# Polysketch attention and a gated feed-forward layer on one core: w_out of the first two blocks narrowed separately, later range limits taken one slot later, and the first keys' features made pair by pair

## The chip, the cores and the metric

The kernel runs on one core of a Trainium2 chip. The metric is the device time of one execution in microseconds (us). A core has five engines that run side by side, each through its own list of instructions in order: PE (TensorE, matrix products into PSUM; its weight loads are a row of their own in the profile, PEld), DVE (VectorE), ACT (ScalarE), POOL (GpSimd) and SP, which issues DMAs here. Engines wait for one another on semaphores.

## The reference

For each of 4 batches and 4 heads there are 1088 tokens with queries, keys and values of 32 numbers. With two small matrices S1 and S2 (8 x 32), features are made: phi(x) holds the 64 products of (S1 x) and (S2 x). Then

```
kv  = sum over tokens of phi(k) v          z = sum over tokens of phi(k)
x   = (phi(q) kv) / (phi(q) z + 1e-6)      heads side by side: 4352 tokens x 128
out = (sigmoid(x w_gate) * (x w_val)) w_out     128 -> 1536 -> 128
```

S1, S2 and the three feed-forward weights arrive as 64-bit floats, q, k and v as 32-bit ones.

## The kernel before

**Attention**, batch by batch. Keys and queries are turned by DVE (turn_k, turn_q). kps makes the sketches of the keys with eight matmuls of 64 x 32 weights: four groups of tokens, and two pairs of heads (pi) in each. Both pairs go into one PSUM tile of two banks (`t[:, pi]`), and DVE turns each pair back into KAB. outer multiplies KAB into the key features KP; for batch 0 gram gets the sum z early, from the products of KAB with itself. kv0 (batch 0) or kv sums kv, and dn makes denominators and numerators; DVE divides and writes xT, the input of the feed-forward layer. A batch's queries come in two parts; the second part's features (batch 0) travel through DRAM (q01, qcomp and spread) and are multiplied by qmult, L630.

**Feed-forward**, over 9 chunks of tokens (512 each, the last 256), and in each over 12 blocks of 128 hidden units. w1 (L351) is a wave: gate and value of one block, 4 passes of 512 columns on PE (L363), then the sigmoid on ACT (L371). glu multiplies the two on DVE (L384), one slot later. w2 (L320, tile moeout) adds the block's share of the output, another slot later. slot (L398) writes this order: the pending glu, the due w2, the next w1. Work of later batches is put into slots of earlier chunks. All orders on PE, DVE, ACT and POOL are the order of the program text.

**Narrowing.** The 64-bit weights are loaded as pairs of words and brought to 32-bit floats on the chip, in the first chunk while the waves run. A block j takes w_gate, w_val and w_out together (384 columns). narrow (L83) is a generator with four steps:

- step 0: POOL limits the high word (L97, tile cap); ACT converts the low word (L101, tile tail)
- step 1: DVE shifts and joins bits of the high word (L105, L109, tile head)
- step 2: ACT squares the limited value (L117, tile square); POOL adds tail to head (L118)
- step 3: DVE writes the weight, with values below a bound set to zero (L127, tile w_sb)

The square goes to a PSUM bank if one is named (`bank`), else it is written over cap in SBUF. Blocks 10 and 11 have no bank. In this text "part" numbers are those of narrow_01 (L187), which narrows blocks 0 and 1: part 0 is gate and value of block 0, part 1 those of block 1, and part 2 is w_out of both blocks at once (256 columns). Parts 0 and 1 and the first steps of part 2 and block 2 stand around the division of the first tokens (head1, L871). The rest is issued by w1 (L372 to L379): in the slot of wave j0 of chunk 0, step 3 of block j0 + 1, steps 1 and 2 of block j0 + 2, and step 0 of block j0 + 4. head1 issues step 0 of blocks 2 and 3.

PSUM tiles are taken by tag: "acc0" and "acc1" (one bank each; output sums, squares and small results), "two" (two banks) and "wave" (two tiles of two banks).

Of the kernel before, what the change touches and what calls it, by code (L numbers as in the profile page):

```python
# [8 lines left out]
F32 = mybir.dt.float32  # L9
# [7 lines left out]
P = 128  # L17
# [3 lines left out]
def kernel(  # L21
# [12 lines left out]
    nc = tc.nc  # L34
# [11 lines left out]
    NJK = 9  # L46
    KBASE = [0, 9, 17, 25]
    assert T == 34
    TCH = 512
# [12 lines left out]
    pso = ctx.enter_context(tc.tile_pool(name="pso", bufs=1, space=bass.MemoryType.PSUM))  # L62
# [112 lines left out]
    def narrow_w(j, step):  # L175
        if not 0 <= j < NJ:
            return
        n, jj = divmod(j, 2)
        if wide:
            if step == 0:  # L180
                narrowing[j] = narrow(
                    w_sb[:, :, j, :], w_in[n][:, :, jj], nc.gpsimd, "acc1" if j < NJ - 2 else None
                )
            next(narrowing[j])


    def narrow_01(part, step):  # L187
        if wide:
            if step == 0:
                i = (slice(0, 2), part) if part < 2 else (2, slice(0, 2))  # L190
                narrowing["01", part] = narrow(
                    w_sb[:, i[0], i[1]],
                    w_in[0][:, i[0], i[1]],
                    nc.gpsimd,
                    "acc0" if part else "acc1",
                )
            next(narrowing["01", part])

# [81 lines left out]
    for c in range(2):  # L280
        rows = slice(64 * c, 64 * c + 64)
        nc.vector.tensor_reduce(
            out=m_col[rows, c],
            in_=ident[rows].rearrange("p (k j) -> p j k", j=R),
# [3 lines left out]
    for t, x in (  # L288
# [5 lines left out]
        out=e_sum,  # L294
        in_=bass.AP(
            tensor=e_row.tensor,
            offset=e_row.offset,
            ap=[list(e_row.ap[0]), [0, 2], [1, R], [0, R]],
        ),
# [4 lines left out]
    for n in range(2):  # L304
        t = const.tile([P, H, 32], F32, tag=f"zb{n}", name=f"zb{n}")
# [45 lines left out]
    def w1():  # L351

        ci = moe["ci"]
        t0, tw = tok_chk[ci]
        jn = TCH // tw
        j0 = moe["w"] * jn
        wv = psm.tile([P, 2, TCH], F32, tag="wave", name="wave")

        tp = tw // 2 if ci == 0 and j0 == 0 else tw
        for o in range(0, tw, tp):  # L360
            for which in range(2):
                for jj in range(jn):
                    nc.tensor.matmul(  # L363
                        out=wv[:, which, jj * tw + o : jj * tw + o + tp],
                        lhsT=w_sb[:, which, j0 + jj, :],
                        rhs=xT[:, t0 + o : t0 + o + tp],
                        start=True,
                        stop=True,
                    )
        sg = sbG.tile([P, TCH], F32, tag="sg", name="sg", bufs=3)  # L370
        nc.scalar.activation(out=sg, in_=wv[:, 0], func=ACTF.Sigmoid)  # L371
        if ci == 0:  # L372
            if j0 == 1:
                narrow_01(2, 3)
            if 0 < j0 < NJ - 2:
                narrow_w(j0 + 1, 3)
            narrow_w(j0 + 2, 1)
            narrow_w(j0 + 2, 2)
            narrow_w(j0 + 4, 0)  # L379


        def glu():
            g = sbG.tile([P, TCH], F32, tag="g", name="g")
            nc.vector.tensor_tensor(out=g, in0=wv[:, 1], in1=sg, op=MUL)  # L384
            moe["todo"].append((ci, j0, jn, g.rearrange("p (j t) -> p j t", j=jn)))

        moe["gate"] = glu
        moe["w"] += 1
        if j0 + jn == NJ:
            moe["ci"] += 1  # L390
            moe["w"] = 0
# [29 lines left out]
    kT_of, qT_of = {}, {}  # L421
# [22 lines left out]
    KP, QP, BQ, ND, KAB, ASB, KVZ, KVD, Z4, ZS = ({} for _ in range(10))  # L444

    def kps(b):
        t = ps2.tile([P, 2, 512], F32, tag="two", name="kps")
        for g in range(4):
            for pi in range(2):
                rows = slice(64 * pi, 64 * pi + 64)  # L450
                nc.tensor.matmul(  # L451
                    out=t[32 * g : 32 * g + 32, pi, : NJK * 32],
                    lhsT=sk[rows, :],
                    rhs=kT_of[b][rows, KBASE[g] : KBASE[g] + NJK],
                    start=True,
                    stop=True,
                )

        KAB[b] = sbA.tile([P, 2, NJK, 32], F32, tag="kab", name="kab")
        for pi in range(2):  # L460
            nc.vector.transpose(
                out=KAB[b][:, pi].rearrange("p j c -> p (j c)"), in_=t[:, pi, : NJK * 32]
            )
        KP[b] = sbA.tile([P, 2, NJK, 2, F], F32, tag="kp", name="kp")

    def gram():
        t = pso.tile([P, TCH], F32, tag="acc1", name="gram")
        for pi in range(2):  # L470
            for j in range(NJK):
                g = 32 * (j % 4)
                x = KAB[0][: 64 if j == 0 else P, pi, j]
                nc.tensor.matmul(  # L474
                    out=t[g : g + 32, 32 * pi : 32 * pi + 32],
                    lhsT=x,
                    rhs=x,
                    start=(j < 4),
                    stop=(j >= NJK - 4),
                    skip_group_check=True,  # L480
                )
        gs = const.tile([P, 2, 2, 2, R], F32, tag="gs")
        nc.scalar.copy(out=gs.rearrange("p a m x r -> p (a m x r)"), in_=t[:, :64])
        gh = const.tile([P, 2, 2, R], F32, tag="gh")
        nc.gpsimd.tensor_tensor(
            out=gh,
            in0=gs[:, :, :, 1],
            in1=bass.AP(
                tensor=e_m.tensor,
                offset=e_m.offset,  # L490
                ap=[list(e_m.ap[0]), [0, 2], [1, 2], [0, R]],
            ),
            op=MUL,
        )

        def spread_z():
            nc.tensor.matmul(
                out=t[:, 64 : 64 + H * R],
                lhsT=e_sum.rearrange("p c i j -> p (c i j)"),
                rhs=gh.rearrange("p a m r -> p (a m r)"),  # L500
                start=True,
                stop=True,
            )

        def mask_z():
            zm = const.tile([P, H, 2, R], F32, tag="zm")
            z0 = t[:, 64 : 64 + H * R]
            nc.vector.tensor_tensor(
                out=zm,
                in0=bass.AP(  # L510
                    tensor=z0.tensor, offset=z0.offset, ap=[list(z0.ap[0]), [R, H], [0, 2], [1, R]]
                ),
                in1=bass.AP(
                    tensor=m_col.tensor,
                    offset=m_col.offset,
                    ap=[list(m_col.ap[0]), [0, H], [R, 2], [1, R]],
                ),
                op=MUL,
            )
            nc.vector.tensor_reduce(  # L520
                out=zb[0][:, :, :2], in_=zm, axis=mybir.AxisListType.X, op=ALU.add
            )

        return spread_z, mask_z
# [268 lines left out]
    else:  # L793
        nc.vector.tensor_copy(
            out=s4[:, 1:],
            in_=bass.AP(
                tensor=s4.tensor, offset=s4.offset, ap=[list(s4.ap[0]), [0, 3], [1, D]]
            ),
# [5 lines left out]
        out=st_[:, : 2 * R],  # L804
        lhsT=s4.rearrange("p g d -> p (g d)"),
        rhs=ident[: 2 * R, : 2 * R],
        is_transpose=True,
        start=True,
        stop=True,
# [3 lines left out]
    sk = const.tile([P, 2, 2, R], F32, tag="sk")  # L813
    nc.vector.tensor_tensor(
        out=sk,
# [11 lines left out]
    sk = sk.rearrange("p m n r -> p (m n r)")  # L827
    sab = []
    for n, inner in enumerate(([[1, R], [0, R]], [[0, R], [1, R]])):
        t = const.tile([P, R, R], F32, tag=f"s{n}", name=f"s{n}")  # L830
        s0 = st_[:, n]
        nc.scalar.copy(
            out=t, in_=bass.AP(tensor=s0.tensor, offset=s0.offset, ap=[list(s0.ap[0])] + inner)
        )
        sab.append(t.rearrange("p i j -> p (i j)"))
    sa, sb = sab
    turn_q(0, 0)
    kps(0)
    ab((0, 0, 0))
    ab((0, 1, 0))  # L840
    spread_z, mask_z = gram()
    mult00 = ab(None, (0, 0, 0))
    mult10 = ab(None, (0, 1, 0), (psm, "wave"))
    for part in range(2):
        narrow_01(part, 0)
# [25 lines left out]
    def head1():  # L871
        narrow_01(1, 1)
        narrow_01(0, 3)
        narrow_01(1, 2)
        narrow_01(2, 0)
        narrow_w(2, 0)
        narrow_w(3, 0)

    divide((0, 4), (4, 8), between=head1)
    narrow_01(1, 3)  # L880
    narrow_01(2, 1)
# [5 lines left out]
    def begin(b):  # L887
        glu()
        kps(b)
        cq[b] = qcomp(b, (0, 1), (psm, "wave"))  # L890
        spread(b, (0, 1), cq[b], nc.sync, nc.gpsimd)
# [76 lines left out]
```

## Time and profile before

| | |
|---|---|
| median of 10 runs | 305.85 us (305.39 to 308.95) |
| the profiled execution | 305.39 us |
| its span, first to last instruction | 303.6 us |
| granted TensorE clock | 1.00 throughout |
| PE passes begin without a gap at the wave's cadence from | 15.2 us |
| last matmul ends | 299.8 us |
| HBM traffic | 19.80 MB read, 3.26 MB written |

Busy time by stretch of the span (us):

| stretch | length | PE | DVE | ACT | POOL |
|---|---|---|---|---|---|
| 0 to 15.2: attention of the first tokens | 15.20 | 12.23 | 12.56 | 6.45 | 4.22 |
| 15.2 to 20.5: the first waves | 5.30 | 4.69 | 4.93 | 3.15 | 3.64 |
| 20.5 to 46: rest of chunk 0, narrowing | 25.50 | 25.50 | 21.37 | 13.10 | 13.45 |
| 46 to 100 | 54.00 | 54.00 | 34.29 | 12.66 | 4.60 |
| 100 to 200 | 100.00 | 100.00 | 50.97 | 22.81 | 8.72 |
| 200 to 303.6 | 103.60 | 99.75 | 30.96 | 22.69 | 0.00 |

A matmul of 512 columns in 32-bit floats is two passes, and each pass is one instruction of the profile; two passes overlap, so a busy PE can still lose time between their starts. The page gives busy times and shares, the chain of work that ended last, groups of instructions, and DMA issues; timelines and lists of waits come from the same trace. "Idle before" is the time an engine stood still ahead of an instruction, and the name behind the arrow is what ended it.

### The profile page before, as it was taken

The numbers are of one execution on the slowest core, as the hardware profiler recorded it, in microseconds if no ns is written. First come the engines' busy times: TensorE is split into PE (matmuls) and PEld (weight loads), VectorE is DVE, ScalarE is ACT, GpSimd is POOL, SyncE is SP. The second block draws the span as 40 slices with busy tenths as digits, with TensorE's granted clock in tenths as the row PEclk, the third lists the DMA queues.
The fourth block names the chain that finished last, engine by engine and source line by source line (L and its number), as shares of the span: only waits on it lengthen the run. The fifth ranks groups of instructions, "written<-read, shape, count | busy, mean of one in ns | idle before, by whom it ended". The sixth has DMA issues, their size and how long they took to land.

```text
span 303.6 us, 3614 instructions
## 1 busy us (share of the span) xinstructions
PE 296.2 (98%) x1366; PEld 136.8 (45%) x1366; DVE 155.1 (51%) x267; ACT 80.9 (27%) x150; POOL 34.6 (11%) x63
## 2 busy tenths in 40 slices
PE   7899999999999999999999999999999999999994
PEld 3444434444344445434444445434444444444683
DVE  6997798756556443464465443635232223222331
ACT  3556532222222222221222222221222222222220
POOL 1365540600000500000004000000000000000000
PEclk9999999999999999999999999999999999999999
DMA  7993440896002490450015940200010000100011
GB/s 222 320 342 88 134 145 4 195 211 202 3 11 60 104 197 15 84 179 0 0 20 118 170 78 2 36 2 0 0 26 9 0 0 10 27 0 0 9 28 17
DMA packets 29586, 23.31 MB, mean 77 GB/s; under 512 B 20928, under 2 KB 24512, under 8 KB 29568
## 3 DMA queue, kind: packets, MB, share of 16 engines
q1 hardware_dynamic: 25200, 15.21, 18.4%
q0 software_dynamic: 3456, 7.09, 11.8%
q10 hardware_dynamic: 912, 0.77, 0.9%
q8 instruction: 11, 0.18, 0.3%
q14 instruction: 7, 0.06, 0.1%
HBM read 19.80 MB, written 3.26 MB: 76 GB/s over the span
## 4 chain that ended last, share of the span: by engine, by line
PE 94%; DVE 2%; DMA 1%; issue 1%; ACT 0%; SPq 0%; DVEq 0%
PE wave L363 57%; PE moeout L320 30%; PE nps L749 2%; PE dps L730 2%; PE kvz L652 1%; PE kps L451 1%; DMA s_in<-in_S_dram 1%; PE cqps L597 1%; PE kvz L638 0%; DVE head L109 0%; PE ndps L708 0%; DVE head L105 0%; DVE kT L428 0%; PE gram L474 0%; DVE w_sb L127 0%
## 5 line engine op out<-in xcount | busy, mean ns | idle before, releaser
L363 PE MATMUL wave<-xT,w_sb 128*128 128x512 f32 (+1 forms) x436 | 191.7, 565 | 0.0
L384 DVE TENSOR_TENSOR g<-wave,sg 128x512 f32<-128x512 f32 x102 | 70.4, 690 | 131.2 <-ACT sg L371 130.9
L363 PEld LDWEIGHTS wave<-xT,w_sb 128*128 128x128 f32 x436 | 82.7, 190 | 93.2 <-issue 87.2
L371 ACT ACTIVATE sg<-wave 128x512 f32<-128x512 f32 x102 | 60.9, 597 | 200.2 <-PE wave L363 198.1
L320 PE MATMUL moeout<-g,w_sb 128*128 128x512 f32 (+1 forms) x216 | 105.5, 576 | 0.6 <-DVE w_sb L127 0.6
L320 PEld LDWEIGHTS moeout<-g,w_sb 128*128 128x128 f32 x216 | 39.6, 190 | 44.1 <-issue 38.4
L621 POOL DMA_DIRECT2D qp<-dq x12 | 7.0, 587 | 109.6 <-DMA dq<-cq 109.6
L118 POOL TENSOR_TENSOR head<-head,tail 128x384 int32<-128x384 int32 (+2 forms) x14 | 13.4, 954 | 18.7 <-DVE head L109 15.7
L530 DVE TENSOR_TENSOR kp<-kab 128x1152 f32<-128x1152 f32 (+2 forms) x10 | 10.8, 1096 | 0.0
L630 DVE TENSOR_TENSOR qp<-qp,bq 128x1152 f32<-128x1152 f32 (+1 forms) x7 | 9.0, 1292 | 0.0
L109 DVE SCALAR_TENSOR_TENSOR head<-cap,head 128x384 int32<-128x384 int32 (+2 forms) x14 | 7.5, 535 | 0.5
L127 DVE SCALAR_TENSOR_TENSOR w_sb<-square,head 128x384 f32<-128x384 f32 (+1 forms) x11 | 5.7, 519 | 3.7 <-POOL head L118 3.7
L330 DVE STREAM_TRANSPOSE o_sb<-moeout 128x512 f32<-128x512 f32 (+1 forms) x9 | 6.1, 681 | 2.6 <-PE moeout L320 2.5
L621 POOL DMA_DIRECT2D bq<-dq x12 | 6.9, 576 | 0.5 <-DVE g L384 0.2
L261 PE MATMUL warm<-ones 128*128 128x512 f32 (+2 forms) x12 | 6.0, 617 | 1.0 <-DVE hm L267 1.0
L101 ACT ACTIVATE tail<-w_in 128x384 int32<-128x384 uint32 (+1 forms) x13 | 6.5, 526 | 0.1
L97 POOL TENSOR_SCALAR cap<-w_in 128x384 f32<-128x384 f32 (+1 forms) x13 | 6.5, 505 | 0.0
L776 DVE TENSOR_TENSOR xT<-nps,rb 128x576 f32<-128x576 f32 (+2 forms) x9 | 5.9, 661 | 0.7
L765 DVE STREAM_TRANSPOSE rb<-rc 128x576 f32<-128x576 f32 (+2 forms) x9 | 6.1, 681 | 0.3
L749 PE MATMUL nps<-qp,nd 64*32 64x256 f32 (+1 forms) x128 | 5.5, 401 | 0.4 <-ACT nd L721 0.4
L439 DVE STREAM_TRANSPOSE qT<-kq 128x512 f32<-128x512 f32 (+1 forms) x8 | 5.7, 716 | 0.0
L730 PE MATMUL dps<-qp,zb 128*32 128x256 f32 (+1 forms) x64 | 5.3, 404 | 0.2 <-DVE zb L520 0.2
(73 smaller groups left out, 83.4 us busy)
## 6 DMA issues: line engine op xcount, KB each, us to landing
qp<-dq POOLq DMA_DIRECT2D x12, 288.0 KB, 8.3
bq<-dq POOLq DMA_DIRECT2D x12, 288.0 KB, 8.6
v<-in_v_dram SPq DMA_DIRECT2D x16, 144.0 KB, 5.1
kq<-in_k_dram SPq DMA_DIRECT2D x3, 544.0 KB, 3.8
kq<-in_q_dram SPq DMA_DIRECT2D x3, 544.0 KB, 4.9
w_in<-in_moe_w_gate_dram SPq DMA_DIRECT2D x6, 256.0 KB, 6.1
w_in<-in_moe_w_val_dram SPq DMA_DIRECT2D x6, 256.0 KB, 5.7
w_in<-in_moe_w_out_dram SPq DMA_DIRECT2D x6, 256.0 KB, 7.2
```

The source lines that it names most:

```text
L97: eng.tensor_scalar(out=cap.bitcast(F32), in0=hi.bitcast(F32), scalar1=122880.0, scalar2=-122880.0, op0=ALU.min, op1=ALU.max,)
L109: nc.vector.scalar_tensor_tensor(out=head, in0=cap, scalar=-0x40000000, in1=head, op0=ALU.bitwise_and, op1=ALU.bitwise_or)
L118: nc.gpsimd.tensor_tensor(out=head, in0=head, in1=tail, op=ALU.add)
L320: nc.tensor.matmul(out=moe["acc"][:, :tw], lhsT=w_sb[:, 2, j, :], rhs=g[:, jj, :tw], start=(j == 0), stop=(j == NJ - 1),)
L363: nc.tensor.matmul(out=wv[:, which, jj * tw + o : jj * tw + o + tp], lhsT=w_sb[:, which, j0 + jj, :], rhs=xT[:, t0 + o : t0 + o + tp], sta ...
L371: nc.scalar.activation(out=sg, in_=wv[:, 0], func=ACTF.Sigmoid)
L384: nc.vector.tensor_tensor(out=g, in0=wv[:, 1], in1=sg, op=MUL)
L530: nc.vector.tensor_tensor(out=KP[b][:, pi, j0:j1].rearrange("p j m (i l) -> p (j m) i l", i=R), in0=bass.AP(tensor=a0.tensor, offset=a0.of ...
L621: get.dma_start(out=t[64 * c : 64 * c + 64, n * H * W1 : (n + 1) * H * W1], in_=bass.AP(tensor=d0.tensor, offset=d0.offset, ap=rows + [[1, ...
L630: nc.vector.tensor_tensor(out=q0, in0=q0, in1=half(BQ[b], n), op=MUL)
L730: nc.tensor.matmul(out=dps[32 * h : 32 * h + 32, :w], lhsT=zb[b % 2][:, h, :], rhs=half(QP[b], n)[:, 2 * (h % 2) + h // 2, :], start=True, ...
L749: nc.tensor.matmul(out=t[32 * h : 32 * h + 32, c, :w], lhsT=ND[b][rows, 32 * h : 32 * h + 32], rhs=half(QP[b], n)[rows, 2 * (h % 2) + h // ...
```

## The change

- narrow_01 has four parts. Part 2 is now w_out of block 0 (128 columns, square in acc0), part 3 w_out of block 1 (128 columns, no bank, so its square is written over cap).
- In w1, step 0 of part 3 follows wave 0, steps 1 and 2 follow wave 1 (after step 3 of block 2, ahead of steps 1 and 2 of block 3), and step 3 follows wave 2, ahead of step 3 of block 3.
- Step 0 of block 3 and up is issued one slot later: block j0 + 3 in the slot of wave j0. head1 no longer issues that of block 3. So on POOL the cap of a block now comes after L118 of the block before it, and no longer after that of two blocks before it.
- kps of batch 0 puts the second pair into a tile of its own, in acc1, makes all four matmuls of the first pair before those of the second, and each transpose waits for its pair. gram takes acc0 instead of acc1.

```diff
     def narrow_01(part, step):
         if wide:
             if step == 0:
-                i = (slice(0, 2), part) if part < 2 else (2, slice(0, 2))
+                j = part % 2
+                i = (slice(0, 2) if part < 2 else slice(2, 3), j)
                 narrowing["01", part] = narrow(
                     w_sb[:, i[0], i[1]],
                     w_in[0][:, i[0], i[1]],
                     nc.gpsimd,
-                    "acc0" if part else "acc1",
+                    ("acc1", "acc0", "acc0", None)[part],
                 )
...
             if j0 == 1:
                 narrow_01(2, 3)
+            if j0 == 2:
+                narrow_01(3, 3)
             if 0 < j0 < NJ - 2:
                 narrow_w(j0 + 1, 3)
+            if j0 == 1:
+                narrow_01(3, 1)
+                narrow_01(3, 2)
             narrow_w(j0 + 2, 1)
             narrow_w(j0 + 2, 2)
-            narrow_w(j0 + 4, 0)
+            if j0 == 0:
+                narrow_01(3, 0)
+            narrow_w(j0 + 3, 0)
...
     def kps(b):
         t = ps2.tile([P, 2, 512], F32, tag="two", name="kps")
-        for g in range(4):
-            for pi in range(2):
...
+        ts = [t[:, 0], t[:, 1]]
+        turns = [(g, pi) for g in range(4) for pi in range(2)]
+
+        if b == 0:
+            ts[1] = pso.tile([P, TCH], F32, tag="acc1", name="kps1")
+            turns.sort(key=lambda x: x[1])
+        for g, pi in turns:
+            rows = slice(64 * pi, 64 * pi + 64)
+            nc.tensor.matmul(
+                out=ts[pi][32 * g : 32 * g + 32, : NJK * 32],
...
             nc.vector.transpose(
-                out=KAB[b][:, pi].rearrange("p j c -> p (j c)"), in_=t[:, pi, : NJK * 32]
+                out=KAB[b][:, pi].rearrange("p j c -> p (j c)"), in_=ts[pi][:, : NJK * 32]
             )
...
     def gram():
-        t = pso.tile([P, TCH], F32, tag="acc1", name="gram")
+        t = pso.tile([P, TCH], F32, tag="acc0", name="gram")
...
         narrow_01(2, 0)
         narrow_w(2, 0)
-        narrow_w(3, 0)
```

## The prediction

> **What bounds the kernel now.** I read the page's busy times first, then the chain that ended last, then the timelines of PE, DVE and POOL where PE stalls. On the page:
>
> ```profile
> PE 296.2 (98%) x1366; PEld 136.8 (45%) x1366; DVE 155.1 (51%) x267; ACT 80.9 (27%) x150; POOL 34.6 (11%) x63
> ...
> PE 94%; DVE 2%; DMA 1%; issue 1%; ACT 0%; SPq 0%; DVEq 0%
> ```
>
> PE is the bound: the chain lies on it for 94%. In the trace, a 512-wide matmul pass follows the one before after 0.429 us from 15.21 us to the end, apart from fixed steps at changes of shape (0.52 and 0.53). A change pays only if it moves the start of this cadence, or takes a hole out of it. There are two holes. The PE timeline shows the first (a line gives start, length, engine, code line, operation and tiles; in brackets the idle time before and what ended it):
>
> ```profile
> 19.54 1.12 PE L320 MATMUL moeout<-g,w_sb 128*128 128x512 f32 x2 [0.61 <-DVE w_sb L127]
> 20.50 1.88 PE L363 MATMUL wave<-xT,w_sb 128*128 128x512 f32 x4
> ```
>
> The last pass of wave 1 starts at 18.330, so moeout 0 was due at 18.759. It starts at 19.535, and its first pass holds PE 0.533 instead of 0.429: the hole is 0.776 + 0.104 = 0.88 us. Its weights came from DVE at 19.481, so data that DVE ends at t are usable at t + 0.158 (19.481 to 18.759 + 0.88). The second hole is in the weight loads:
>
> ```profile
> 45.92 0.30 PEld L363 LDWEIGHTS wave<-xT,w_sb 128*128 128x128 f32 x2 [0.63 <-DVE w_sb L127]
> ```
>
> L127 of block 11 ends at 45.866; + 0.158 is 46.024, and the wave was due at 45.955: 0.07 us. So the narrowing, not PE, is the tighter of the two at 46 us. Between the holes it runs as a ring, L118 on POOL, L127, L105, L109 on DVE, L118: L127 of blocks 4 and 5 start at 25.00 and 27.62, 2.62 us a block, where PE takes 2.575 (six passes). **Whatever reaches L127 of block 11 is what the kernel pays**; a gain in PE before that is lost there.
>
> DVE and POOL around the first hole:
>
> ```profile
> 16.21 0.56 DVE L105 TENSOR_SCALAR head<-cap 128x256 int32<-128x256 int32 x1
> 16.80 0.42 DVE L109 SCALAR_TENSOR_TENSOR head<-cap,head 128x256 int32<-128x256 int32 x1
> ...
> 17.53 1.02 DVE L109 SCALAR_TENSOR_TENSOR head<-cap,head 128x384 int32<-128x384 int32 x1
> 18.47 0.68 DVE L384 TENSOR_TENSOR g<-wave,sg 128x512 f32<-128x512 f32 x1
> 19.07 0.41 DVE L127 SCALAR_TENSOR_TENSOR w_sb<-square,head 128x256 f32<-128x256 f32 x1
> 19.75 0.56 DVE L127 SCALAR_TENSOR_TENSOR w_sb<-square,head 128x384 f32<-128x384 f32 x1 [0.27 <-POOL head L118]
> ...
> 21.09 0.77 DVE L439 STREAM_TRANSPOSE qT<-kq 128x576 f32<-128x576 f32 x1
> ```
>
> ```profile
> 17.40 0.73 POOL L118 TENSOR_TENSOR head<-head,tail 128x256 int32<-128x256 int32 x1 [0.78 <-DVE head L109]
> 18.72 1.00 POOL L118 TENSOR_TENSOR head<-head,tail 128x384 int32<-128x384 int32 x1 [0.59 <-DVE head L109]
> 19.68 0.53 POOL L97 TENSOR_SCALAR cap<-w_in 128x384 f32<-128x384 f32 x1
> ```
>
> L109 takes 1.02 beside POOL's L118 and 0.56 elsewhere; L105 takes 0.56 beside a cap (16.08 to 16.62) and 0.25 elsewhere. Taking off their usual times, the one began at 17.99 and the other at 16.52, 0.14 and 0.10 before POOL's recorded ends (18.13, 16.62). **These two wait POOL out.** L127 at 19.75 reads its square from PSUM, overlaps a cap, and takes its usual 0.56.
>
> **Part 1, pair by pair.** The passes of two quads of such matmuls end 0.03 us apart (the aps pair: 7.343 and 7.374). So the first kab transpose starts 0.03 earlier, and DVE and PE follow up to the first wave. Bounds: -0.05 (the first record of kps ends at 6.643, the last at 6.694) and +0.25 (two quads in series, as the gram quads are). I take -0.03, the nearest row. The changed banks cost nothing: what held acc0 was read by 6.3, and gram needs it at 7.3.
>
> **Part 2, the first hole.** For 128 columns I carry on the slope of 256 and 384: L105 0.253, 0.351, so 0.16; L109 0.426, 0.558, so 0.29; L127 0.413, 0.558, so 0.27; L118 0.728, 0.997, so 0.46; cap 0.29. DVE begins part 2 (w_out of block 0) at 16.19. The third cap of before no longer lies there, so: L105 to 16.35, L109 to 16.68, L105 of block 2 to 16.95. L118 of part 2 runs 16.85 to 17.31, and L109 of block 2 waits it out for 0.21: to 17.75, 0.80 earlier. Then g of wave 0 waits for its sigmoid (17.81) and ends at 18.52, and L127 of part 2 at 18.72. moeout 0 can run at 18.875, due at 18.73. **PE is 0.77 ahead** of its 19.645 (this working gives 19.645 where the trace has 19.639). L127 of block 2 ends at 19.52, in time for wave 2.
>
> **Part 3, what is given back.** (a) Part 3 (w_out of block 1) now stands on DVE before block 3: L105 waits out the cap of block 3 (to 19.67) and ends at 19.71, L109 at 20.04, L105 of block 3 at 20.31; L118 of part 3 holds POOL 20.22 to 20.68, and L109 of block 3 waits again, to 21.11. From L127 of block 2 this takes 1.60, against 0.86 before: 0.74 of the 0.80 is gone. qT ends at 21.81 (21.86 before), so cqps, due at 21.54, runs at 21.86: stall 0.32. (b) L127 of part 3 waits behind g of wave 1 (to 22.41). It has no bank, so both its inputs are in SBUF; right before it, POOL, freed by L118 of block 3 at 22.29, starts the cap of block 4 (22.25 to 22.78). I let it wait that out: end 22.94, not 22.60. moeout 1 can run at 23.10, due 22.48: stall 0.62. PE is now 0.17 behind, with wave 3 and all that follows queued there. Also L127 of block 3, queued on DVE, starts at 22.86 instead of 22.40 in the same working of before: +0.46. (c) The cap of each later block now comes after the L118 before it, so L105 waits for it: cap end + 0.034 (the lag of L127 behind L118, 24.964 to 24.998), 0.02 a block later. Six blocks: +0.10. (d) At block 10 the same meets an L127 without a bank:
>
> ```profile
> 39.45 1.35 DVE L630 TENSOR_TENSOR qp<-qp,bq 128x1152 f32<-128x1152 f32 x1
> 40.72 0.68 DVE L384 TENSOR_TENSOR g<-wave,sg 128x512 f32<-128x512 f32 x1
> 41.69 0.56 DVE L127 SCALAR_TENSOR_TENSOR w_sb<-cap,head 128x384 f32<-128x384 f32 x1 [0.29 <-POOL head L118]
> ...
> 45.35 0.52 DVE L127 SCALAR_TENSOR_TENSOR w_sb<-cap,head 128x384 f32<-128x384 f32 x1
> ```
>
> Now POOL is idle at 41.69, since the cap of block 11 was made at 38.05. After the change this cap follows L118 of block 10 at once, 0.07 before L127 is released: +0.35. DVE has no idle time from there to L127 of block 11. Sum there: 0.46 + 0.10 + 0.35 = +0.91.
>
> No row shows an L127 without a bank beside POOL work. Bounds for each of (b) and (d): 0 (L127 at 19.75 beside a cap) and +0.46 (L109 beside L118). I take 0.34 and 0.35, as L105 waited for a cap.
>
> The Trainium skill (SBUF — State Buffer, "SBUF: two separate sides") speaks against this change: a DVE instruction with two SBUF inputs and a GpSimd instruction exclude each other for a whole instruction, and the first one wins. By it each L127 would lose up to a full cap, an estimate of 0.5, and the time would be about 307.0.
>
> Counted at nothing: ACT's tail and square of part 3 (0.30 and 0.29), beside waves 1 and 2, when ACT is idle from 19.56 to 20.34; without that room each would delay a sigmoid by as much. No DMA is added or moved. POOL's own issues (from 54.77) stand behind the narrowing, which ends 10 us before them.
>
> **The sum.** Block 11's L127 is 0.91 late, PE meets it, and the hole there grows from 0.07. After it nothing makes PE wait, so the end moves as much: span 303.6 + 0.9 = 304.5, and 305.39 + 0.9 = 306.3 for the profiled execution. The median of the 10 runs is 0.46 above that execution: 306.75, about **306.7**, 0.3% slower.
>
> **Rivals.** *Gain kept* (13%): if PE and not the ring sets the time at 46 us, the first hole goes: at most -0.88, so 305.0. For it: 0.9 us of slack at block 4. Against: 0.09 at block 11. *No waiting out in (b), (d) or both* (17%): +0.91 less 0.34, 0.35 or 0.69, so 306.1 to 306.5. For it: L127 at 19.75. Against: L109 at 17.53. *Gain and loss cancel, or the early order changes nothing* (8%): 305.85. *Slower by more than 0.5%* (7%): the hand-over of the cap to L105, eight times on the ring. I price it with the 0.034 of POOL to DVE. The way back, L109 to L118, takes 0.175 (26.416 to 26.591); at that price each block costs 0.14 more, 8 x 0.14 = 1.1, so 307.9. It passes the bound from about 0.08 a block on. *Forecast* (55%): 306.4 to 307.2.
>
> **How the numbers follow.** A measurement tells about 0.5% (1.5 us) from no change. 305.3 to 307.5 leaves out the slow rival and most of the gain, 2 in 10 or a little less. Faster by over 0.5% needs more than the two holes hold: 0.02. Slower: the slow rival and the far end of the forecast, 0.08. Within: 0.90.
>
> **What would show it.** moeout 0 near 18.9; cqps stalled near 21.9; L127 of part 3 and of block 10 taking about 0.6 and 0.9 instead of 0.27 and 0.56; the ring at 2.64; the weight load of wave 11 idle before L127 near 46.8. If PE shows no hole near 47, or block 10's L127 takes 0.56, I am wrong.

## The result and the profile after

| | before | after |
|---|---|---|
| median | 305.79 us (305.30 to 308.95, 53 runs) | 306.75 us (306.26 to 310.27, 15 runs) |
| profiled execution | 305.39 us | 306.53 us |
| its span | 303.6 us | 304.8 us |

The ratio is 1.0041, with a 95% interval of 1.0021 to 1.0060: slower by 0.96 us between the medians, by 1.14 us between the profiled executions, and inside the 0.5% that the prediction set as its bound. Some executions of most kernels here take 2 to 4 us longer than the others of the same kernel, and medians hold their share of these, a large one in e7_both and e10_early_cap.

The page of after has the same bound as before, with a chain that is longer off PE:

```profile
PE 297.0 (97%) x1366; PEld 136.7 (45%) x1366; DVE 156.0 (51%) x270; ACT 81.2 (27%) x152; POOL 35.0 (11%) x65
...
PE 83%; DMA 6%; DVE 5%; POOL 3%; issue 1%; ACT 0%; POOLq 0%; SPq 0%; DVEq 0%
```

PE fell from 94% of the chain to 83%; POOL came in with 3%, all of it L118, and DVE rose from 2% to 5%: the chain that ends last now runs through the narrowing, and before that the input loads (DMA), until it reaches PE for good. PE's timeline shows where it crosses. First the region of the hole that the change aims at:

```profile
18.72 1.12 PE L321 MATMUL moeout<-g,w_sb 128*128 128x512 f32 x2
19.68 1.88 PE L364 MATMUL wave<-xT,w_sb 128*128 128x512 f32 x4
21.88 0.69 PE L610 MATMUL cqps<-qT,skq 64*32 64x288 f32 x8 [0.32 <-DVE qT L447]
23.00 1.13 PE L321 MATMUL moeout<-g,w_sb 128*128 128x512 f32 x2 [0.43 <-DVE w_sb L127]
```

moeout 0 has lost its wait (it stood 0.61 idle before, at 19.54). PE then stands idle at two other places, 0.32 before cqps and 0.43 before moeout 1. And at the other end of the narrowing, the weight load of wave 11:

```profile
47.06 0.30 PEld L364 LDWEIGHTS wave<-xT,w_sb 128*128 128x128 f32 x2 [1.37 <-DVE w_sb L127]
```

The weight load waits 1.37 us where it waited 0.63; PE itself stands idle 0.54 there. Behind it PE has no hole up to the end. So the starts of L127 along the narrowing tell the whole difference:

| L127 of block | before | after | difference |
|---|---|---|---|
| 2 | 19.752 | 18.951 | -0.80 |
| 3 | 22.376 | 22.870 | +0.49 |
| 9 | 38.112 | 38.765 | +0.65 |
| 10 | 41.692 | 42.390 | +0.70 |
| 11 | 45.349 | 46.489 | +1.14 |

The gain of 0.80 is made, is gone within one block (1.29 us lost between blocks 2 and 3), and then more is lost in two ways: slowly along the ring, and at once behind block 10. The last line equals the 1.14 us between the two profiled executions.

DVE around part 3, with POOL beside it:

```profile
20.40 0.74 DVE L109 SCALAR_TENSOR_TENSOR head<-cap,head 128x384 int32<-128x384 int32 x1
21.06 0.77 DVE L447 STREAM_TRANSPOSE qT<-kq 128x576 f32<-128x576 f32 x1
...
22.33 0.62 DVE L127 SCALAR_TENSOR_TENSOR w_sb<-cap,head 128x128 f32<-128x128 f32 x1
22.87 0.54 DVE L127 SCALAR_TENSOR_TENSOR w_sb<-square,head 128x384 f32<-128x384 f32 x1
```

```profile
20.27 0.45 POOL L118 TENSOR_TENSOR head<-head,tail 128x128 int32<-128x128 int32 x1 [0.59 <-DVE head L109]
...
22.27 0.53 POOL L97 TENSOR_SCALAR cap<-w_in 128x384 f32<-128x384 f32 x1
```

Read the durations against the shapes. L109 of block 3 takes 0.74 beside L118 of part 3, 0.56 elsewhere. L127 of part 3, with a third of the columns (square written over cap, so both inputs in SBUF), takes 0.62, while L127 of block 3 with three times the columns, behind the end of that cap, takes 0.54. So the recorded start of such a DVE line need not be the start of its work: the reading is that it sits behind POOL's cap until that ends (the experiments test this). The same at block 10, on DVE and on POOL:

```profile
42.39 1.00 DVE L127 SCALAR_TENSOR_TENSOR w_sb<-cap,head 128x384 f32<-128x384 f32 x1 [0.29 <-POOL head L118]
...
46.49 0.52 DVE L127 SCALAR_TENSOR_TENSOR w_sb<-cap,head 128x384 f32<-128x384 f32 x1
```

```profile
42.32 0.65 POOL L97 TENSOR_SCALAR cap<-w_in 128x384 f32<-128x384 f32 x1
```

The cap of block 11 begins 0.07 ahead of L127 of block 10, which takes 1.00 instead of 0.56.

### The profile page after: what moved, and what is told of

The parts are those of the page before. It is cut to its first block, busy times and chain, and to the rows that moved or that the text cites. A ratio compares the mean times of both kernels' runs of the same rounds, so it can differ in the third digit from the quotient of the medians.

```text
span 304.8 us, 3627 instructions
## 1 busy us (share of the span) xinstructions
PE 297.0 (97%) x1366; PEld 136.7 (45%) x1366; DVE 156.0 (51%) x270; ACT 81.2 (27%) x152; POOL 35.0 (11%) x65
## 4 chain that ended last, share of the span: by engine, by line
PE 83%; DMA 6%; DVE 5%; POOL 3%; issue 1%; ACT 0%; POOLq 0%; SPq 0%; DVEq 0%
PE wave L364 51%; PE moeout L321 27%; POOL head L118 3%; DMA w_in<-in_moe_w_val_dram 2%; DMA v<-in_v_dram 2%; DVE w_sb L127 2%; DVE head L109 1%; PE kvz L665 1%; PE nps L762 1%; PE dps L743 1%; DMA w_in<-in_moe_w_gate_dram 1%; DMA kq<-in_k_dram 1%; DVE head L105 1%; PE kps L464 1%; PE cqps L610 0%
## 5 line engine op out<-in xcount | busy, mean ns | idle before, releaser
L118 POOL TENSOR_TENSOR head<-head,tail 128x384 int32<-128x384 int32 (+3 forms) x15 | 13.5, 901 | 19.5 <-DVE head L109 16.6
L109 DVE SCALAR_TENSOR_TENSOR head<-cap,head 128x384 int32<-128x384 int32 (+3 forms) x15 | 7.5, 503 | 0.5
L127 DVE SCALAR_TENSOR_TENSOR w_sb<-square,head 128x384 f32<-128x384 f32 (+2 forms) x11 | 5.6, 506 | 3.9 <-POOL head L118 3.9
L101 ACT ACTIVATE tail<-w_in 128x384 int32<-128x384 uint32 (+2 forms) x14 | 6.8, 499 | 1.1 <-DMA w_in<-in_moe_w_out_dram 1.1
L97 POOL TENSOR_SCALAR cap<-w_in 128x384 f32<-128x384 f32 (+2 forms) x14 | 6.8, 490 | 0.3 <-DMA w_in<-in_moe_w_out_dram 0.3
```

The costliest lines, as they stand in the source:

```text
L109: nc.vector.scalar_tensor_tensor(out=head, in0=cap, scalar=-0x40000000, in1=head, op0=ALU.bitwise_and, op1=ALU.bitwise_or)
L118: nc.gpsimd.tensor_tensor(out=head, in0=head, in1=tail, op=ALU.add)
L127: nc.vector.scalar_tensor_tensor(out=out, in0=square, scalar=1.265625 * 2.0**-30, in1=head, op0=ALU.is_ge, op1=MUL)
```

## The experiments

The theory after the result is the prediction's: the gain at the first hole is real, DVE and POOL give it back around part 3, and L127s without a bank lose a cap's time twice. One thing differs: the first wave starts 0.10 earlier, not 0.03 (15.115 against 15.212). The rivals: the pairs or the bank swap carry a gain of their own that the rest hides; a cap that stands right behind L118 costs by its semaphore hand-over and not by excluding DVE; the later caps cost nothing. In this section "ring" is the time between L127 starts of two blocks in the profile. Every kernel was run beside the kernel before on the same chip. Where there is one execution alone, its steps are read and not its time.

**e1_pairs: the kernel before with only the pair by pair part.**

```
-        t = pso.tile([P, TCH], F32, tag="acc1", name="gram")
+        t = pso.tile([P, TCH], F32, tag="acc0", name="gram")
(and the whole kps hunk of the change)
```

> The kernel before with the change to kps and gram alone (second pair in a tile of its own, gram in acc0). Theory (the narrowing sets the time from 16 to 46 us, and everything that starts it earlier moves the end as much): the first wave starts 0.10 earlier, L127 of block 11 ends 0.10 earlier (45.77 instead of 45.87), the time falls by 0.1 us (0.03%), which only the profile can show. Most of it comes from dps, which no longer waits for gram's own bank: it starts 0.05 after zb instead of 0.15. Rival (the pairs in turn are the gain): 0.07 earlier already at the first kab transpose, and that much kept up to the first wave.

Measured: median 305.54 us (305.36 to 306.43, 12 runs) against 305.89 us, ratio 0.9984 (0.9968 to 1.0001): no difference that this measurement can tell. In the profile the first transpose of kab does start 0.07 earlier behind kps (0.756 against 0.824), but at the end of zb nothing is left of it (4.70 to 4.71 behind the first kps in before, after and e1_pairs). The first wave is not early: kvz, which takes v as weights, started 0.19 behind the end of dps, because the last part of v landed only at 11.334 (11.165 before). The expected earlier L127 of block 11 was missed (45.364 against 45.349). That is informative: with a first wave 0.17 later than before's (15.384 against 15.212), L127 of block 11 moved by 0.015. With the three caps of the kernel before in POOL, L127 of block 2 starts 5.23 to 5.24 us after the start of L118 of part 1 in before, e1_pairs, e2_gram and e4_cap11 alike; the first wave's start does not reach it. In the changed kernel POOL has less to do there: it is 4.46, and L105 of part 2 takes 0.26 beside a cap (0.22 in e6_p3_early, with no POOL instruction beside it), so a part of an early start can count.

**e2_gram: the kernel before with only the bank of gram changed.**

```
-        t = pso.tile([P, TCH], F32, tag="acc1", name="gram")
+        t = pso.tile([P, TCH], F32, tag="acc0", name="gram")
```

> The kernel before with gram in acc0 and kps unchanged. Theory: dps starts 0.05 after zb instead of 0.15, the first wave 0.09 earlier, although no kab transpose is earlier. Rival (the pairs in turn are the gain): no change at the first wave, 15.21.

Measured: one execution, 306.43 us; its inputs arrived about 1 us late, so only steps count. Before, then e2_gram, from the timelines of all engines:

```profile
10.46 0.22 DVE L520 TENSOR_REDUCE zb<-zm 128x8 f32<-128x64 f32 x1
...
10.83 0.64 PE L730 MATMUL dps<-qp,zb 128*32 128x256 f32 x8 [0.24 <-DVE zb L520]
```

```profile
11.49 0.22 DVE L520 TENSOR_REDUCE zb<-zm 128x8 f32<-128x64 f32 x1
...
11.77 0.64 PE L730 MATMUL dps<-qp,zb 128*32 128x256 f32 x8 [0.21 <-DVE zb L520]
```

From the end of zb to dps it is 0.146 before (10.681 to 10.827) and 0.056 here (11.715 to 11.771), with the pairs untouched. So the bank, and not the pairs, brings the earlier dps: 0.09. The trace shows the step: with gram in acc1 a semaphore instruction of 0.05 us stands on PE's queue ahead of the weight load of dps, with gram in acc0 there is none. That it is there for PE's own gram in the same bank is the reading of the program.

That this makes the first wave of the changed kernel earlier does not follow, and other rows speak against it. kvz behind dps waits for v. SP's issue of w_in at 11.18 waits for the landing of the last part of v, and tells when it came. Before, then after:

```profile
11.18 0.38 SPq L168 DMA_DIRECT2D w_in<-in_moe_w_out_dram  x1
...
11.41 1.48 PE L638 MATMUL kvz<-kp,v 128*32 128x64 f32 x72
```

```profile
11.09 0.38 SPq L168 DMA_DIRECT2D w_in<-in_moe_w_out_dram  x1
...
11.31 1.48 PE L651 MATMUL kvz<-kp,v 128*32 128x64 f32 x72
```

v landed at 11.165 and at 11.068, and kvz starts 0.246 behind it in both: the 0.10 of the first wave is the 0.10 of the landing. The change does not touch that load, and its landing moves from execution to execution (10.24 in e6_p3_early, 11.67 in e3_caps). Where v was there before zb ended, the first wave comes 4.40 behind zb with gram in acc0 (e2_gram, e6_p3_early, e7_both) and 4.40 to 4.41 with gram in acc1 (e8_spare_cap, e9_spare_memset). So no gain of the bank is seen at the first wave.

**e3_caps: the kernel before with only the caps from block 3 one slot later.**

```
-            narrow_w(j0 + 4, 0)
+            narrow_w(j0 + 3, 0)
...
-        narrow_w(3, 0)
```

> The kernel before with every cap from block 3 on one slot later, and nothing else. Theory (ports): the third cap no longer delays L105 of blocks 0 and 1, so moeout 0 is 0.28 earlier (about 19.36) and so is L127 of block 3; then 0.02 to 0.035 a block is lost, and 0.35 to 0.45 at block 10, where L127 takes 0.9 to 1.0 instead of 0.56: L127 of block 11 ends 0.2 to 0.4 late, the time rises by 0.2 to 0.4 us. Rival (PE alone sets the time): the 0.28 is kept, the time falls by 0.28. Rival (the hand-over of the cap costs 0.14 or more a block): over 1 us slower.

Measured: median 306.05 us (305.62 to 308.45) against 305.89 us, ratio 0.9999 (0.9978 to 1.0020). Its profile has the losses: the ring takes 0.044 more a block from block 3 to 9 (0.02 to 0.035 were expected), L127 of block 10 takes 0.997, and from block 2 to 11 the ring takes 26.40 instead of 25.60. The gain of 0.28 at the first hole can't be read from it: v landed late (11.673), the first wave stands at 15.72, 0.51 later than before, and moeout 0 at 19.77, 0.23 later. The net that the theory expects, -0.28 and +0.80, is 0.5; the medians differ by 0.16, and the interval of about 0.6 to either side holds both. Of its time nothing can be said, of its steps the losses alone.

**e4_cap11: the kernel before with only the cap of block 11 one slot later.**

```
-            narrow_w(j0 + 4, 0)
+            if j0 + 4 < NJ - 1:
+                narrow_w(j0 + 4, 0)
+            if j0 + 3 == NJ - 1:
+                narrow_w(NJ - 1, 0)
```

> The kernel before with the cap of block 11 alone one slot later, so that POOL makes it beside L127 of block 10, whose inputs both lie in SBUF. Theory (ports): that L127 takes 0.9 to 1.0 instead of 0.56, and L127 of block 11, PE's hole near 46 and the end move by 0.35 to 0.45. Rival (only the hand-over from POOL to DVE counts): L127 of block 10 takes 0.56, L105 of block 11 starts at most 0.03 late, the end does not move.

Measured: one execution, 306.11 us. L127 of block 10 takes 0.992, and the ring from block 10 to 11 takes 4.09 instead of 3.66: +0.43 from one moved cap.

**e8_spare_cap and e9_spare_memset: is it the wait or the port?** In e4_cap11 L105 of block 11 also waits for the moved cap. e8_spare_cap leaves all caps where they were and adds one more of the same shape at that place, which nobody reads; e9_spare_memset puts there a POOL instruction of nearly the same length that reads nothing.

```
             narrow_w(j0 + 2, 2)
+            if j0 == NJ - 4:
+                spare = sbN.tile([P, 3, P], F32, tag="spare", name="spare")
+                nc.gpsimd.tensor_scalar(
+                    out=spare,
+                    in0=w_in[5][:, :, 1, :, 1].bitcast(F32),
+                    scalar1=122880.0, scalar2=-122880.0, op0=ALU.min, op1=ALU.max,
+                )
```
```
             narrow_w(j0 + 2, 2)
+            if j0 == NJ - 4:
+                spare = sbN.tile([P, 512], F32, tag="spare", name="spare")
+                nc.gpsimd.memset(spare, 0.0)
```

> The kernel before with one more POOL instruction: the cap of block 11 made a second time, right behind L118 of block 10, into a tile that nothing reads. No instruction waits for it. Theory (ports): L127 of block 10 takes 0.9 to 1.0 instead of 0.56 and the end moves by 0.35 to 0.45. Rival (a wait for the cap is what costs): 0, for nothing waits.

> The same place, but the POOL instruction is a memset of 512 columns (about 0.5 us), which writes SBUF and reads nothing; nothing reads it. By the Trainium skill (SBUF — State Buffer, SBUF: two separate sides), a DVE instruction with two SBUF inputs is shut out only by a GpSimd instruction that reads SBUF: L127 of block 10 would take its 0.56 and the end would stay. Rival (any busy POOL shuts it out): 0.9 to 1.0, the end 0.35 later.

Measured: 306.06 us with the spare cap, 305.53 us with the memset, one execution each. POOL, then DVE, of e8_spare_cap:

```profile
41.75 0.65 POOL L381 TENSOR_SCALAR spare<-w_in 128x384 f32<-128x384 f32 x1
```

```profile
41.82 1.00 DVE L127 SCALAR_TENSOR_TENSOR w_sb<-cap,head 128x384 f32<-128x384 f32 x1 [0.29 <-POOL head L118]
```

and of e9_spare_memset:

```profile
41.74 0.51 POOL L381 MEMSET spare<- 128x512 f32 x1
```

```profile
41.83 0.56 DVE L127 SCALAR_TENSOR_TENSOR w_sb<-cap,head 128x384 f32<-128x384 f32 x1 [0.29 <-POOL head L118]
```

Both POOL instructions lie over the start of L127. Beside the one that reads SBUF, L127 takes 1.00 and block 11 comes 0.44 later (ring 4.10, against 3.66); beside the one that only writes, it takes 0.56 and nothing moves (3.66). Nothing on DVE waits for the result of either of them. So it is not a wait for data; the two differ in that one reads SBUF (and in the operation, which no run holds fixed). The Trainium skill (SBUF — State Buffer, "SBUF: two separate sides") says just this: an instruction of VectorE with two SBUF inputs is shut out only by a GpSimd instruction that reads SBUF, and the first one to start has the port that the two engines share to its end. The runs agree with 0.56 and 1.00, except that the first one is not left alone either: the cap itself takes 0.65 there, against 0.53 elsewhere. Two inputs are not the only case: L105 has one SBUF input, and takes 0.56 beside a cap in the kernel before and 0.25 with no POOL instruction beside it.

**e5_caps_back: the changed kernel with the caps in their old slots.**

```
-            narrow_w(j0 + 3, 0)
+            narrow_w(j0 + 4, 0)
...
+        narrow_w(3, 0)
```

> The changed kernel with the caps back in their old slots (j0 + 4, block 3 in head1); w_out of blocks 0 and 1 stays apart. Theory: of the 1.14 us that block 11's L127 lost in the changed kernel, about 0.6 comes back (0.44 at block 10, 0.17 over the six blocks before it, less some 0.15 for a third cap beside L105 at the start): the last hole of PE is at about 46.5, the time 0.5 to 0.6 below the changed kernel's, still 0.5 above the one before. Rival (the split of w_out is what costs): 0.1 or less comes back.

Measured: median 306.33 us (306.01 to 309.88) against 305.65 us, ratio 1.0026 (0.9994 to 1.0058). The profiled execution starts late (last section), so the ring is read. It is 15.73 from block 3 to 9 (15.90 in after, 15.74 before) and 3.66 from block 10 to 11, and L127 of block 10 takes 0.559: from block 2 to 11, 0.68 of ring are back. L127 of part 3 still takes 0.590, since the cap of another block stands beside it then. The medians of this kernel and of after differ by 0.42, in the right direction (0.5 to 0.6 were expected), but come from different chips, and the interval of the ratio includes 1.

**e6_p3_early: the changed kernel with L127 of part 3 right behind L109 of block 3.**

```
-            if j0 == 2:
-                narrow_01(3, 3)
...
+            if j0 == 1:
+                narrow_01(3, 3)      (behind narrow_w(j0 + 2, 2), ahead of the cap)
```

> The changed kernel with L127 of part 3 right behind L109 of block 3, ahead of qT and of the cap of block 4. Theory (ports): it takes 0.28 instead of 0.62, L127 of block 3 and all after it start 0.34 earlier, moeout 1 at about 22.7 instead of 23.0, and the time is 0.3 below the changed kernel's. Rival (only its place in DVE's order costs): qT is 0.2 later, moeout 1 and the end stay.

Measured: one execution, 306.27 us, 0.26 under the profiled execution of after. DVE, then PE:

```profile
21.13 0.28 DVE L127 SCALAR_TENSOR_TENSOR w_sb<-cap,head 128x128 f32<-128x128 f32 x1
```

```profile
22.15 0.69 PE L610 MATMUL cqps<-qT,skq 64*32 64x288 f32 x8 [0.49 <-DVE qT L447]
22.77 1.12 PE L321 MATMUL moeout<-g,w_sb 128*128 128x512 f32 x2
```

The instruction that took 0.62 beside a cap takes 0.28 once none is there, moeout 1 waits for nothing, and the ring from block 2 to 3 is 3.58 instead of 3.92. What it costs is to be seen in the same lines: qT comes behind it, and cqps waits 0.49 instead of 0.32.

**e7_both: the changed kernel with both of these edits.**

> The changed kernel with both repairs: caps in their old slots, and L127 of part 3 ahead of qT and of the next cap. Theory (the two losses are separate and add): from L127 of block 2 to that of block 11 it takes 27.54 - 0.68 - 0.34 = 26.5 us, against 25.6 in the kernel before; block 2 itself is 0.8 earlier than before; so the end lies within 0.2 us of the kernel before, and what the split of w_out wins at the first hole is all spent by its own extra instructions on the ring. Rival (the split is a gain once the ports are kept clear): 0.5 us or more faster than before.

Measured: median 306.52 us (305.54 to 309.81) against 305.66 us, ratio 1.0041 (1.0009 to 1.0073); its profiled execution took 305.54 us, span 303.8. Six of its 12 times lie at 305.54 to 306.07, one at 306.97 and five above 308. Of the 23 times of the kernel before, 18 lie at 305.16 to 305.94. The ring from block 2 to 11 is 26.52, as expected, against 25.60 before and 27.54 after. With both repairs the split of w_out wins nothing: L127 of block 11 starts 39.64 after the first kps, before 39.38 (39.40 in e9_spare_memset). The two profiled executions lie 0.15 apart, as expected (0.2); the medians lie 0.86 apart, so by them neither the 0.2 nor a gain over the changed kernel, whose ratio is 1.0041 too, is shown.

**e10_early_cap: e1_pairs with the cap and tail of part 2 (both blocks' w_out at once) made earlier, while POOL is idle.** The edit moves `narrow_01(2, 0)` from head1 to behind the activation that prepares the first division.

> The kernel of e1 (pairs in turn, gram in acc0; w_out of blocks 0 and 1 together, caps in their old slots), with the cap and the tail of part 2 made while POOL and ACT are idle (11.7 to 12.9 us) instead of behind head1. Theory: POOL then has two caps, not three, ahead of L105 of part 2, which takes 0.25 instead of 0.56; moeout 0, L127 of block 2 and L127 of block 11 come 0.3 earlier than in e1, and nothing is added on the ring: the time falls by 0.2 to 0.4 us against the kernel before. Rivals: the cap delays kp or L105 of part 0 by as much on DVE (0); its data land too late in some runs and ACT's tail holds up kvd (slower by 0.1 to 0.3).

Measured: median 305.68 us (305.02 to 308.13) against 305.66 us, ratio 1.0016 (0.9990 to 1.0043). L105 of part 2 now meets only the end of a cap (0.28 instead of 0.56), but L127 of block 2 stands at 19.77, 0.02 later than before, with a first wave 0.30 later. The first of the rivals shows in the profile, the early cap beside kp:

```profile
10.78 1.52 DVE L535 TENSOR_TENSOR kp<-kab 128x512 f32<-128x512 f32 x2
11.19 0.55 POOL L97 TENSOR_SCALAR cap<-w_in 128x256 f32<-128x256 f32 x1 [1.11 <-DMA w_in<-in_moe_w_out_dram]
```

kp has two SBUF inputs, and its two instructions take 1.52 instead of 1.28; 0.18 of the first wave's delay is there at the first kps already. Counted from the first kps, L127 of block 11 is still 0.13 earlier than before (39.24 against 39.38). The gain of 0.2 to 0.4 that was expected is not shown in the time; seven of its 12 times lie at 305.02 to 305.79 and five above 307.4, so it is not excluded either. No version clearly beats both kernels.

## Why the prediction was right, step by step

**The bound.** "Whatever reaches L127 of block 11 is what the kernel pays" holds to 0.01 us: L127 there is 1.14 late, and so is the end. The rival *gain kept* is refuted by the load of wave 11, idle 1.37. *No waiting out* is refuted by the 0.62 and the 1.00 of the two L127s. *Gain and loss cancel* falls with the interval, whose lower end is 1.0021.

**Pair by pair** was put at -0.03 with "the changed banks cost nothing". The first wave came 0.10 earlier (15.115 against 15.212), and that is luck: v landed 0.10 earlier in the profiled execution of after, and kvz waits for v (e2_gram). The prediction carried the earlier kab through DVE and PE to the first wave; the 0.07 of kab is gone at zb, and v's load is not in its chain. It asked when acc0 was free for gram, and did not ask who waits for the bank that gram leaves: the 0.09 at dps are such a wait, though they did not reach the first wave.

**The first hole.** L127 of part 2 was put at an end of 18.72 and ended at 18.665; PE was to be 0.77 ahead and was 0.82. Two misses nearly cancelled up to L109 of block 2 (17.75 in both): the earlier start, and 0.10 in L105 of 128 columns, 0.26 and not 0.16. Of these, 0.06 is the straight line through 256 and 384 columns (0.22 in e6_p3_early, with no POOL instruction beside it); the rest is a cap that still lay beside it, to 16.30. The last 0.05 is the sigmoid of wave 0, which came earlier with the first wave. The prediction's "0.25 elsewhere" for L105 passes over the one at 13.44, which takes 0.46 beside an L118; it fits the same reading.

**Given back around part 3.** L109 of block 3 was put at 21.11 and ended at 21.13; cqps at 21.86 and came at 21.88; L127 of part 3 at 22.94 and ended at 22.946; moeout 1 at 23.10 and, with the 0.10 that its first pass was held, was usable at 23.10. Block 3 is 0.49 late, against 0.46. That L127 of part 3 waits out a cap is shown by e6_p3_early: 0.62 beside it, 0.28 without.

**The hand-over of the caps** was put at 0.02 a block, from a lag of 0.034 between POOL's end and L105. The lines of block 5:

```profile
28.07 0.53 POOL L97 TENSOR_SCALAR cap<-w_in 128x384 f32<-128x384 f32 x1
```

```profile
28.14 0.56 DVE L127 SCALAR_TENSOR_TENSOR w_sb<-square,head 128x384 f32<-128x384 f32 x1 [0.60 <-POOL head L118]
28.64 0.36 DVE L105 TENSOR_SCALAR head<-cap 128x384 int32<-128x384 int32 x1
```

The lag is as put: L105 starts 0.034 behind the cap's end. It starts 0.502 behind the start of L127, where it was 0.475, and takes 0.36 instead of 0.35: on the ring, 2.657 a block against 2.623. From block 3 to 10 that is 0.20 us, predicted 0.10. The rival at 0.14 a block is refuted: L105 waits for POOL at POOL's price to DVE, and the way back was in the ring already. These lines also show what a bank is worth: this L127 lies beside a cap as block 10's does, has its square in PSUM, and takes 0.56.

**L127 of block 10** was put at 0.9, +0.35. It took 1.00, +0.44: right in mechanism (e4_cap11, e8_spare_cap, e9_spare_memset), too small because the cap it waits out was itself longer, 0.65 instead of 0.53. The prediction's other estimate, 0.5 for each L127, is nearer here and too much at part 3 (0.34). It gives its rule for any POOL instruction; by e9_spare_memset it does not hold for one that only writes, and a cap reads SBUF.

**The sum.** +0.91 was forecast and +1.14 measured between the profiled executions: 0.03 at part 3, 0.10 in the hand-over, 0.09 at block 10. The median came out at 306.75 for a forecast of 306.7, closer than the sum deserves: the prediction carried the old execution's 0.46 to the median over, and for after it is 0.22, while over more runs the kernel before came to 305.79. And the luck of v makes the measured loss smaller than the change's own, by 0.10 at most.

**Open.** Why the cap at block 10 stretches to 0.65 when the one at part 3 keeps 0.53, with an L127 shut out in both places. Why the ring of e3_caps loses 0.044 a block and that of after 0.034. The times of e3_caps, e7_both and e10_early_cap.

## What to carry to other kernels

When the bound engine has several holes that one supply chain sets, a gain at the first is worth only what it leaves at the last: follow the chain to the next place where PE waits before a gain is counted. When a POOL instruction is moved, look at which DVE instruction it comes to lie beside; here those with two SBUF inputs waited out a POOL instruction that reads SBUF, and were saved by a PSUM operand, by a place ahead of it, or by leaving the POOL instruction where DVE has no such instruction (an idle POOL is not enough, as e10_early_cap shows). For a tile that changes banks, list who waits for the old bank as well as for the new one. And before a start that came earlier is credited to a change, look when its input data landed.

## What the runs showed of the hardware that was not expected

With gram in another bank than before, dps, which waits for DVE's zb in both kernels, starts 0.09 us earlier behind it (0.056 instead of 0.146), though gram had ended about 1 us before. Of the 0.09, 0.05 is the semaphore instruction that is gone.

The first matmuls of the profiled execution of e5_caps_back (308.24 us) are slow. The groups of PE by shape between 5 and 9 us, e5_caps_back and then before (busy time, mean ns of one):

```profile
L464 PE MATMUL kps<-kT,sk 64*32 64x288 f32 x16 | 1.2, 685 | 0.0
```

```profile
L451 PE MATMUL kps<-kT,sk 64*32 64x288 f32 x16 | 0.7, 415 | 0.0
```

685 against 415 ns, a factor of 1.65, and its first wave starts at 17.50 instead of 15.12 in after; 0.33 of this is there at the first kps already (6.30 against 5.97). The granted clock reads 1.00 in both executions, so the profile does not name the cause. The Trainium skill (TensorE: Matmul & The Clock Gate, "Part 1: The HAM clock gate (the "warmup" mystery)") tells of a clock that is let through at half rate until the array has been busy for a while, at a moment that varies from run to run, and puts the loss at under 1% of a typical span; the 2.1 us left here are 0.7%, which would agree in size, but no row here shows that clock.
